# Second layer of two experts with 288 tokens: weights stationary, tokens moving, outputs transposed back on TensorE

## The chip, the cores and the metric

The kernel runs on 1 core of a Trainium2 chip. The metric is device time in microseconds (us) of one execution. Three runs of the kernel before took 524.7, 527.82 and 528.58 us; the median, 527.82, is its time.

## The reference, cut to what matters

Causal attention with 4 sink positions and a window of 128 over 4 batches, 8 heads, 768 positions and head size 64 gives x, 3072 tokens of 512 features. Then comes a mixture of experts: each token goes to one of 4 groups and in it to one of 4 experts, by the largest logit, so to one of 16.

```python
for g in range(G):            # 4 groups
    ...
    for e in range(Eg):       # 4 experts in each
        h = np.maximum(xg[mask_e] @ w1[g, e], 0.0)   # 512 -> 1024
        ye = h @ w2[g, e]                            # 1024 -> 512
        combined = g_w[mask_g][mask_e] * e_w[mask_e]
        out[tok_idx] = combined[:, None] * ye
```

Inputs and outputs are float32.

## The kernel before, in words

The first part of the span is attention and routing. From some 170 us on the experts are computed, in an order that depends on their load: an expert has a rank r by its number of tokens, and the rank has a fixed capacity, `CAPT[r]` (L44): 384, 256, 480, 288, 288, 224, ... tokens. Ranks 3 and 4 have 288. `GROUPS` (L49) pairs each with a small rank, its mate in this text: [3, 14] with 288 and 64 tokens, [4, 15] with 288 and 32. The group after each of them is one rank with 160 tokens (8 and 9). `PARTS` (L66) adds to each the offset `o`, the number of 128-token blocks `nt` (3 for 288), and `s`, the size of a rest of at most 64 tokens (32 for 288).

Every float32 product is made from three: each operand is split in a rounded part (hi) and a residual (lo), and hi x hi, hi x lo and lo x hi are added up. Weights arrive by DMA in chunks of 512 KB into `rw` (5 buffers); `wjob` (L668) casts one to `whi` on ScalarE and makes `wlo` on VectorE. There are 12 pairs of `whi` and `wlo`; a pair can be used again once its chunk has been counted in `state["freed"]`.

Layer 1 of a wide rank (`layer1_wide`, L921) has the weights stationary and the tokens moving: 8 steps of 128 hidden features, into a bank `ph` of PSUM (4 buffers) each. Under 240 tokens hi and lo of the tokens move together, and ScalarE copies half of the bank to `hc` and VectorE adds the other half to it; from 240 on there are three matmuls. `split_h` (L904) applies ReLU and splits the result into `hx` (hi on ScalarE, residual on VectorE). The mate's layer 1 (`layer1_narrow`) has the tokens stationary; its hidden layer `hs` is transposed on TensorE (`hidden_t`) while layer 2 of the large rank runs.

Layer 2 (`layer2`, L1001) has the tokens stationary and the weights moving, 512 columns wide: for each block of 128 tokens 8 steps of three matmuls into a bank `po` (2 buffers); the rest of 32 tokens has hi and lo side by side as 64 stationary columns, and so two matmuls a step. ScalarE scales the result by the gate into `ot` (3 buffers; for the rest VectorE adds the second half), and GpSimd scatters the rows to `out` by an indirect DMA.

The order of all instructions on each engine is the program's. The generators yield an estimate of PE time at each step; `spend` (L880) adds it to a clock and to a credit, and issues a weight cast when the credit reaches 1.8, a free pair is there and the planned landing of the raw chunk has passed. `pop_todo` (L995) issues in layer 2, at planned steps, the transposes of the mate's hidden layer and of the next group's inputs (`xpose`, L890). `fetch` (L1041) issues the gathers of inputs two groups ahead, on GpSimd's queue.

Of the kernel before, what the change touches and what calls it, by code (L numbers as in the profile page):

```python
# [9 lines left out]
F32 = mybir.dt.float32  # L10
# [4 lines left out]
AF = mybir.ActivationFunctionType  # L15
# [6 lines left out]
P = 128  # L22
# [4 lines left out]
DM = H * D  # L27
HP = H // 2
NDC = DM // P
G, EG, F = 4, 4, 1024  # L30
NE = G * EG
NFC = F // P
# [40 lines left out]
for _g in PARTS:  # L73
    _o = 0
    for _q in _g:
        _rem = _q["T"] % P
        _q.update(o=_o, nt=(_q["T"] + P - 1) // P, s=_rem if _rem <= 64 else 0)
        _o += 2 * _q["T"]
MAXB = 6
MAXA = 7  # L80
# [49 lines left out]
def moe_attention(tc, kqT, vN, vS, nsw, wgx, w1, w2, out):  # L130
    nc = Pinned(tc)
    v = nc.vector
    with ExitStack() as top, ExitStack() as att:
# [9 lines left out]
        ps_t = None  # L143
# [5 lines left out]
        def const(shape, dt, name):  # L149
            return cp.tile(shape, dt, name=name)  # L150
# [12 lines left out]
        hx = un[:, NDC * W:(NDC + NFC) * W].rearrange("p (f w) -> p f w", w=W)  # L163
# [3 lines left out]
        def bank(pt):  # L167
            return pt.tile([P, 4, P], F32, name="tp")
# [63 lines left out]
        ident = const([P, P], F32, "ident")  # L232
# [219 lines left out]
        start = const([P, NE], F32, "start")  # L452
# [173 lines left out]
        xg, cg, later = {}, {}, []  # L626
# [15 lines left out]
        state = dict(issued=0, done=0, freed=0, credit=0.0, route=0.0, clk=0.0, at=0.0, dma=0.0, gap=PELAG, dve=0.0)  # L642
# [25 lines left out]
        def wjob(force=False):  # L668
            if tail:
                prefetch(RAW)  # L670
            k = state["done"]
            if raws and not force and state["clk"] < raws[0][4]:
                return None
            if not raws or k >= state["freed"] + WBUF or (k % WBUF >= WA and len(wpool) < 2):
                return None
            l, r, c, rw, _ = raws.pop(0)
            wp = wpool[k % WBUF >= WA]
            hi = wp.tile([P, F], F32R, name="whi")
            lo = wp.tile([P, F], F32R, name="wlo")
            z = F if tail else F // 2  # L680
            nc.scalar.copy(hi[:, 0:z], rw[:, 0:z])

            def rest():
                v.tensor_tensor(lo, rw, hi.bitcast(F32), ALU.subtract)
                wt[l, r, c] = hi, lo
                if tail:
                    prefetch(RAW)
            dve(1.2)
            state["done"] += 1
            if tail:  # L690
                rest()
                return True

            def more():
                nc.scalar.copy(hi[:, z:], rw[:, z:])
                return rest

            half.append(more)
            return None
# [88 lines left out]
        po = ob[1].rearrange("p (c n) -> p c n", c=HP)  # L788
# [86 lines left out]
        def wait_for(key):  # L875
            while key not in ready:
                state["clk"] += 0.3
                routing(1)
# [36 lines left out]
        def weights(*k):  # L915
            while k not in wt:
                if not wjob(True):
                    raise RuntimeError("weights out of order")
            return wt[k]
# [75 lines left out]
        def pop_todo():  # L995
            plan["at"] += 1
            if plan["todo"] and plan["at"] >= plan["next"]:
                plan["next"] += plan["every"]
                plan["todo"].pop(0)()

        def layer2(q, j):  # L1001
            T, o, s, r = q["T"], q["o"], q["s"], q["r"]
            w = min(P, T - j * P)
            st = w if j * P + w > T - s else 0
            po = ps_o.tile([P, DM], F32, name="po")
            lastj = j == q["nt"] - 1
            for f in range(NFC):
                whi, wlo = (t[:, (f % 2) * DM:(f % 2 + 1) * DM] for t in weights(2, r, f // 2))
                hh = hx[:, f, o + j * P:o + j * P + w]
                a, z = f == 0, f == NFC - 1  # L1010
                if st:
                    hb = hx[:, f, o + j * P:o + j * P + 2 * w]
                    if z:
                        nc.tensor.matmul(po[0:w], hh, wlo, start=False, stop=False)
                    nc.tensor.matmul(po[0:2 * w], hb, whi, start=a, stop=z)
                    if not z:
                        nc.tensor.matmul(po[0:w], hh, wlo, start=False, stop=False)
                else:
                    hl = hx[:, f, o + T + s + j * P:o + T + s + j * P + w]
                    nc.tensor.matmul(po[0:w], hh, whi, start=a, stop=False)  # L1020
                    nc.tensor.matmul(po[0:w], hh, wlo, start=False, stop=False)
                    nc.tensor.matmul(po[0:w], hl, whi, start=False, stop=z)
                pop_todo()
                state["freed"] += 1 if q["last"] and lastj and f % 2 else 0
                yield 0.467 if st else 0.7
            jj = q["j0"] + j
            ot = yp.tile([P, DM], F32, name="ot", bufs=3)
            c = cg[r, jj]
            if q is PARTS[-1][-1] and j == 0:
                nc.scalar.activation(ot[:, 0:DM // 2], po[:, 0:DM // 2], AF.Copy, scale=c)  # L1030
                v.tensor_scalar(ot[:, DM // 2:], po[:, DM // 2:], c, None, ALU.mult)
            else:
                nc.scalar.activation(ot[0:w], po[st:st + w], AF.Copy, scale=c[0:w])
            if st:
                v.scalar_tensor_tensor(ot[0:w], po[0:w], c[0:w], ot[0:w], ALU.mult, ALU.add)
            cc = BASE[r] + jj
            nc.gpsimd.indirect_dma_start(
                out=out, out_offset=bass.IndirectOffsetOnAxis(ap=sidx[0:w, cc:cc + 1], axis=0),
                in_=ot[0:w], in_offset=None, bounds_check=N - 1, oob_is_err=False)

        def fetch(nxt):  # L1041
            for q in nxt:
                wait_for(f"x{q['r']}")
                for j in range(q["nt"]):
                    gather(q["r"], q["j0"] + j)

        def finish(g):
            for us in g:
                spend(us)
# [14 lines left out]
        for i in range(NI + 2):  # L1064
            live = i < NI
            a, b = i - 1, i - 2
            mid, old = 0 <= a < NI, 0 <= b < NI
            state["clk"] += 3.0
            if i == NI:
# [5 lines left out]
                ps_h = fl.enter_context(tc.tile_pool(name="ps_h", bufs=4, space=PSUM, side="right", reuse_waits="tile"))  # L1075
# [70 lines left out]
        ps_t = fl.enter_context(tc.tile_pool(name="ps_t", bufs=2, space=PSUM, side="left", reuse_waits="tile"))  # L1146
        ps_o = fl.enter_context(tc.tile_pool(name="ps_o", bufs=2, space=PSUM, side="left", reuse_waits="tile"))

        wpool.append(fl.enter_context(tc.tile_pool(name="wpb", bufs=WB, side="left", reuse_waits="tile")))
        yp = fl.enter_context(tc.tile_pool(name="yp", bufs=2, side="right", reuse_waits="tile"))  # L1150

        for i, g in enumerate(PARTS):
            nxt = PARTS[i + 1] if i + 1 < len(PARTS) else []
            if i == 1:
                fetch(nxt)
            todo = []
            for k, q in enumerate(g):
                plan.update(todo=todo, at=0, next=2, every=2)
                if i == 0 and k == 0:
                    finish(ew)  # L1160
                elif q["T"] > P:
                    finish(layer1_wide(q))
                else:
                    finish(layer1_narrow(q))
                    todo = todo + [lambda q=q, u=u: hidden_t(q, u) for u in range(2)]
            for f in todo if g[0]["T"] <= P else []:
                f()
                todo = []
            tot = NFC * sum(q["nt"] for q in g)
            if i == 0:  # L1170
                todo += [lambda: wait_for("x1"), lambda: None]
            todo += [lambda q=q, j=j: xpose(q, j) for q in nxt for j in range(q["nt"])]
            todo = [lambda fs=todo[k:k + 2]: [f() for f in fs] for k in range(0, len(todo), 2)]
            if i >= 1 and i + 2 < len(PARTS):
                fetch(PARTS[i + 2])
            first = 8 if len(g) > 1 else 2
            plan.update(todo=todo, at=0, next=first, every=(tot - first - 3) / max(1, len(todo)))
            if i == 0:
                plan.update(todo=todo[:1], next=2)
            for q in g:  # L1180
                for j in range(q["nt"])[::1 if i + 1 < len(PARTS) else -1]:
                    finish(layer2(q, j))
                if i == 0 and q["r"] == 0 and not q["last"]:
                    plan.update(todo=todo[1:], next=tot - 8, every=1.5)
            for f in plan["todo"]:
                f()
# [238 lines left out]
```

## Time and profile before

| | |
|---|---|
| median of three runs | 527.82 us |
| profiled execution | 523.2 us, span 521.5 us |
| PE (matmul) busy | 496.1 us, 95% |
| DVE (VectorE) busy | 384.5 us, 74% |
| ACT (ScalarE) busy | 346.9 us, 67% |
| POOL (GpSimd) busy | 157.0 us, 30% |

PE is the row of matmuls, PEld that of weight loads. Matmuls overlap in a pipeline, so a matmul's price is the distance between starts, not the length of its record. In a row "out<-in" the stationary operand of a matmul is shown with its partitions and columns ("128*64"), the moving one with its shape ("128x512"). The releaser of a wait is inferred.

### The profile page before, as it was taken

Reading aid. Unit: us, or ns where it says so; the run is one execution under the profiler, and the core shown is the slowest. Engines: PE = TensorE matmul, PEld = TensorE weight load, DVE = VectorE, ACT = ScalarE, POOL = GpSimd, SP = SyncE. Lnnn points to the kernel's source line nnn. Section 1 sums busy time; section 2 is a strip of 40 time slices with the busy share of each in tenths; the row PEclk is TensorE's granted clock in tenths of the full one; section 3 lists DMA queues with packets and bytes.
Section 4 is the critical chain, followed back from the end, with each engine's and each line's share of the span. In section 5 each row is a group of like instructions: output and inputs, shape, how many; then the busy total and the mean of one; then the engine's idle time right before and its main releaser. Section 6 shows DMA issues by size and latency. Waiting matters only on the chain.

```text
span 521.5 us, 14745 instructions
## 1 busy us (share of the span) xinstructions
PE 496.1 (95%) x5400; PEld 418.8 (80%) x5400; DVE 384.5 (74%) x1184; ACT 346.9 (67%) x900; POOL 157.0 (30%) x272
## 2 busy tenths in 40 slices
PE   8999899899898999999999999999999999999992
PEld 6778778788677988989889869787879797979781
DVE  7466896898987789984175769856988888788640
ACT  4889788798785445772374777755787777687530
POOL 3453453463465011413203021220352031203010
PEclk9999999999999999999999999999999999999996
DMA  7676768688885635895238488858877987598100
GB/s 229 208 209 226 216 195 234 206 277 228 240 265 162 192 121 194 303 318 225 67 105 302 134 263 299 304 165 301 293 253 272 323 288 251 202 314 302 53 5 27
DMA packets 50001, 114.34 MB, mean 219 GB/s; under 512 B 9486, under 2 KB 9486, under 8 KB 49920
## 3 DMA queue, kind: packets, MB, share of 16 engines
q1 hardware_dynamic: 45568, 100.25, 59.9%
q0 software_dynamic: 4352, 13.06, 6.9%
q8 instruction: 45, 0.74, 0.6%
q14 instruction: 36, 0.29, 0.2%
HBM read 100.69 MB, written 13.05 MB: 218 GB/s over the span
## 4 chain that ended last, share of the span: by engine, by line
PE 65%; DVE 1%; ACT 0%; issue 0%; POOL 0%; POOLq 0%; ACTq 0%
PE po L100 33%; PE ph L100 29%; PE tp L100 3%; DVE un L100 0%; DVE wlo L100 0%; ACT whi L100 0%; DVE lt L100 0%; POOL out L100 0%; DVE xt L100 0%; PE lg L100 0%; DVE req L100 0%; ACT xT L100 0%; DVE rm L100 0%; POOLq L1189 0%; DVE ot L100 0%
## 5 line engine op out<-in xcount | busy, mean ns | idle before, releaser
L100 DVE TENSOR_TENSOR wlo<-rw,whi 128x1024 fp32r<-128x1024 f32 x128 | 153.4, 1219 | 35.9 <-ACT whi L100 35.3
L100 PE MATMUL po<-whi,un 128*128 128x512 f32 (+2 forms) x448 | 151.8, 398 | 0.0
L100 ACT CAST whi<-rw 128x1024 fp32r<-128x1024 f32 (+1 forms) x132 | 131.7, 1023 | 18.7 <-DMA rw<-in_w 13.9
L100 PE MATMUL ph<-un,whi 128*128 128x256 f32 (+4 forms) x576 | 131.8, 316 | 0.6 <-DVE un L100 0.5
L100 POOL DMA_INDIRECT out<-ot,sidx x33 | 41.9, 1268 | 241.1 <-ACT ot L100 143.7
L100 PE MATMUL po<-wlo,un 128*128 128x512 f32 (+3 forms) x264 | 103.0, 395 | 0.0
L100 PE MATMUL ph<-un,wlo 128*128 128x160 f32 (+4 forms) x416 | 100.6, 267 | 0.0
L100 PEld LDWEIGHTS po<-whi,un 128*128 128x128 f32 (+2 forms) x448 | 80.3, 179 | 25.1
L100 PEld LDWEIGHTS ph<-un,whi 128*128 128x128 f32 x576 | 94.4, 189 | 2.9 <-DVE un L100 0.7
L100 ACT ACTIVATE pt<-sm,st 128x136 f32<-128x136 f32 x192 | 75.7, 400 | 16.1 <-DVE st L100 16.1
L100 PEld LDWEIGHTS ph<-un,wlo 128*128 128x128 f32 x416 | 77.1, 189 | 0.8
L100 PEld LDWEIGHTS po<-wlo,un 128*128 128x128 f32 (+3 forms) x264 | 43.4, 164 | 14.0
L100 DVE CUSTOM_DVE_ANT_0 sm<-ps,msk 128x136 f32<-128x136 f32 x192 | 45.7, 295 | 5.8 <-PE ps L100 1.8
L100 ACT ACTIVATE ot<-po,cg 128x512 f32<-128x512 f32 (+4 forms) x33 | 22.4, 679 | 34.2 <-PE po L100 25.6
L100 POOL DMA_INDIRECT xg<-xd,gidx x33 | 34.6, 1049 | 32.4 <-DVE key L100 20.8
L100 PE MATMUL ps<-kb,qb 64*64 64x216 f32 (+1 forms) x768 | 38.9, 339 | 1.1 <-DVE st L100 0.9
L100 DVE TENSOR_TENSOR hc<-ph,hc 128x160 f32<-128x160 f32 (+2 forms) x64 | 22.1, 346 | 24.2 <-ACT hc L100 23.9
L100 ACT ACTIVATE un<-ph 128x256 fp32r<-128x256 f32 (+1 forms) x40 | 15.7, 395 | 32.7 <-PE ph L100 32.2
L100 ACT ACTIVATION_READ_ACCUMULATOR pt<-sm,st 128x1 f32 x192 | 36.9, 192 | 0.0
L100 PE MATMUL po<-pa,vv 128*64 128x64 f32 x768 | 31.3, 223 | 3.9 <-issue 3.3
L100 ACT COPY hc<-ph 128x160 f32<-128x160 f32 (+2 forms) x64 | 19.9, 311 | 19.7 <-PE ph L100 12.4
L100 PEld LDWEIGHTS ps<-kb,qb 64*64 64x64 f32 x768 | 26.5, 132 | 7.4 <-DVE st L100 1.4
(190 smaller groups left out, 723.2 us busy)
## 6 DMA issues: line engine op xcount, KB each, us to landing
rw<-in_w SPq DMA_DIRECT2D x128, 512.0 KB, 5.2
vv<-in_vN SPq DMA_DIRECT2D x24, 512.0 KB, 5.8
kb<-in_kqT SPq DMA_DIRECT2D x24, 288.0 KB, 4.5
qb<-in_kqT SPq DMA_DIRECT2D x24, 256.0 KB, 4.0
xd<-xt SPq DMA_DIRECT2D x24, 256.0 KB, 3.6
svr<-in_vS SPq DMA_DIRECT2D x4, 192.0 KB, 4.6
xg<-xd,gidx POOLq DMA_INDIRECT x33, 4.7
out<-ot,sidx POOLq DMA_INDIRECT x33, 5.3
```

Of the source, the lines that this page charges most:

```text
L100: r = f(*a, **k)
```

## The change

Ranks that have between 240 and 384 tokens and a rest over a multiple of 128 get the mark `tr`; only ranks 3 and 4 do. For them `s` is 0, so residuals lie in one stretch, and a new generator, `layer2_cols`, takes the place of `layer2`. It makes the output with features on partitions: 4 passes c over 128 output features, each with 8 steps f of three matmuls with 128 weight columns stationary and 288 tokens moving, into a `ph` bank. ScalarE copies each pass to SBUF; three of these strips lie in an `hs` tile, the fourth in an `ot` tile. Then TensorE transposes 128x128 blocks back, four for each block of tokens (nine of the first three strips, and then three of the fourth), into the two `po` banks and one bank `tp`; ScalarE scales each into `ot`, and GpSimd scatters it. The mate's layer 2 follows in the old form.

```diff
-        _q.update(o=_o, nt=(_q["T"] + P - 1) // P, s=_rem if _rem <= 64 else 0)
+        _q["tr"] = 240 < _q["T"] < 384 and _rem > 0
+        _q.update(o=_o, nt=(_q["T"] + P - 1) // P, s=_rem if _rem <= 64 and not _q["tr"] else 0)
...
+        def layer2_cols(q):
+            T, o, r = q["T"], q["o"], q["r"]
+            yw = yp.tile([P, F], F32, name="hs", bufs=2)
+            yl = yp.tile([P, DM], F32, name="ot", bufs=3)
+            y = [yw[:, c * T:(c + 1) * T] for c in range(NDC - 1)] + [yl[:, 0:T]]
+            for c in range(NDC):
+                ph = ps_h.tile([P, 512], F32, name="ph")
+                for f in range(NFC):
+                    cs = slice(f % 2 * DM + c * P, f % 2 * DM + (c + 1) * P)
+                    whi, wlo = (t[:, cs] for t in weights(2, r, f // 2))
+                    hh, hl = hx[:, f, o:o + T], hx[:, f, o + T:o + 2 * T]
+                    a, z = f == 0, f == NFC - 1
+                    nc.tensor.matmul(ph[:, 0:T], whi, hh, start=a, stop=False)
+                    nc.tensor.matmul(ph[:, 0:T], whi, hl, start=False, stop=False)
+                    nc.tensor.matmul(ph[:, 0:T], wlo, hh, start=False, stop=z)
+                    if (c * NFC + f) % 4 < q["nt"]:
+                        pop_todo()
+                    state["freed"] += 1 if c == NDC - 1 and f % 2 else 0
+                    yield 0.4
+                nc.scalar.copy(y[c], ph[:, 0:T])
+            tx = [ps_o.tile([P, DM], F32, name="po").rearrange("p (a b) -> p a b", a=NDC) for _ in range(2)]
+            tx.append(bank(ps_t))
+            ws = [min(P, T - j * P) for j in range(q["nt"])]
+            for cs in (range(NDC - 1), range(NDC - 1, NDC)):
+                for j, w in enumerate(ws):
+                    for c in cs:
+                        nc.tensor.transpose(tx[j][0:w, c], y[c][:, j * P:j * P + w], ident)
+            for j, w in enumerate(ws):
+                ot = yp.tile([P, DM], F32, name="ot", bufs=3)
+                c = cg[r, q["j0"] + j]
+                nc.scalar.activation(ot[0:w], tx[j][0:w].rearrange("p a b -> p (a b)"), AF.Copy, scale=c[0:w])
+                scatter(r, q["j0"] + j, w, ot)
+            yield 1.2
...
             for q in g:
+                if q["tr"]:
+                    finish(layer2_cols(q))
+                    continue
                 for j in range(q["nt"])[::1 if i + 1 < len(PARTS) else -1]:
                     finish(layer2(q, j))
```

`scatter` is the indirect DMA that stood at the end of `layer2`, made a function.

## Rows read from the trace of the kernel before

**Rows 1.** The page, parts 1 and 2: busy time; granted clock in 40 slices

```profile
PE 496.1 (95%) x5400; PEld 418.8 (80%) x5400; DVE 384.5 (74%) x1184; ACT 346.9 (67%) x900; POOL 157.0 (30%) x272
...
PEclk9999999999999999999999999999999999999996
```

**Rows 2.** The chain of waits from 235 us on: shares by line

```profile
by line: PE po L100 48.8%; PE ph L100 43.2%; PE tp L100 4.7%; POOL out L100 0.3%; POOLq L1189 0.2%; DVE ot L100 0.2%; ACT ot L100 0.2%; issue 0.0%
```

**Rows 3.** Windows: length, busy time (count) of PE, PEld, DVE, ACT, POOL; clock, DMA

```profile
293.41:310.07 16.66, 16.66 (x81) 12.18 (x80) 12.13 (x17) 11.40 (x16) 1.29 (x1) 1.00 0.82 272
310.07:313.81 3.74, 3.74 (x18) 2.58 (x17) 3.74 (x5) 3.61 (x5) 1.72 (x1) 1.00 0.85 226
313.81:322.36 8.55, 8.55 (x66) 8.33 (x64) 7.92 (x21) 5.67 (x17) 0.89 (x1) 1.00 0.97 359
349.82:366.50 16.68, 16.68 (x82) 12.14 (x81) 11.88 (x17) 11.27 (x16) 1.68 (x2) 1.00 0.84 272
```

**Rows 4.** Timeline of PE (start, length): layer 1 of rank 4, first, next layer's first

```profile
333.30 0.43 PE L100 MATMUL ph<-un,whi 128*128 128x288 f32 x2
...
346.10 0.40 PE L100 MATMUL ph<-whi,un 128*64 128x512 f32 x1
```

**Rows 5.** Transposes: mean length of a record by form; eight together in PE's timeline

```profile
L100 PE MATMUL tp<-ident,xg 128*128 128x128 f32 x72 | 10.1, 272 | 0.0
...
306.83 0.95 PE L100 MATMUL tp<-ident,xg 128*128 128x128 f32 x8
307.72 0.44 PE L100 MATMUL po<-whi,un 128*64 128x512 f32 x1
```

**Rows 6.** Timeline of ACT, both groups (in brackets: idle before, and releaser)

```profile
285.07 0.41 ACT L100 ACTIVATE un<-ph 128x288 fp32r<-128x288 f32 x1 [1.19 <-PE ph L100]
...
305.69 0.69 ACT L100 ACTIVATE ot<-po,cg 128x512 f32<-128x512 f32 x1 [2.92 <-issue]
...
310.91 2.93 ACT L100 CAST whi<-rw 128x1024 fp32r<-128x1024 f32 x3
314.05 0.69 ACT L100 ACTIVATE ot<-po,cg 64x512 f32<-64x512 f32 x1 [0.22 <-ACT whi L100]
...
355.99 1.05 ACT L100 CAST whi<-rw 128x1024 fp32r<-128x1024 f32 x1 [2.20 <-DMA rw<-in_w]
```

**Rows 7.** The tile ot: landing of its scatters; POOL's timeline, both groups

```profile
DMA to landing us min/median/max: 2.2/5.3/7.7
...
303.04 1.29 POOL L100 DMA_INDIRECT out<-ot,sidx  x1 [17.88 <-ACT ot L100]
310.98 1.72 POOL L100 DMA_INDIRECT out<-ot,sidx  x1 [6.64 <-ACT whi L100]
318.68 0.89 POOL L100 DMA_INDIRECT out<-ot,sidx  x1 [5.98 <-DVE un L100]
324.19 0.92 POOL L100 DMA_INDIRECT out<-ot,sidx  x1 [4.62 <-DVE un L100]
...
359.43 1.30 POOL L100 DMA_INDIRECT out<-ot,sidx  x1 [16.95 <-ACT ot L100]
366.12 2.96 POOL L100 DMA_INDIRECT out<-ot,sidx  x1 [5.39 <-ACT whi L100]
```

**Rows 8.** Timeline of DVE: layer 1 of rank 8 and what is before it

```profile
315.81 0.73 DVE L100 SCALAR_TENSOR_TENSOR ot<-po,cg,ot 64x512 f32<-64x512 f32 x1
316.47 0.30 DVE L100 TENSOR_TENSOR hc<-ph,hc 128x160 f32<-128x160 f32 x1
...
318.05 0.32 DVE L100 TENSOR_TENSOR hc<-ph,hc 128x160 f32<-128x160 f32 x1
...
320.85 0.32 DVE L100 TENSOR_TENSOR hc<-ph,hc 128x160 f32<-128x160 f32 x1
```

**Rows 9.** Timeline of PE: the same layer 1, a usual pair and the last step

```profile
318.80 0.49 PE L100 MATMUL ph<-un,whi 128*128 128x320 f32 x2
...
320.88 0.75 PE L100 MATMUL ph<-un,whi 128*128 128x320 f32 x2
```

More of the change, by code (lines that the diff above doesn't have):

```diff
@@ L1035, in layer2, with scatter @@
                 v.scalar_tensor_tensor(ot[0:w], po[0:w], c[0:w], ot[0:w], ALU.mult, ALU.add)
+            scatter(r, jj, w, ot)
+        def layer2_cols(q):
[31 more added lines that the diff above has]
+            yield 1.2
+        def scatter(r, jj, w, ot):
             cc = BASE[r] + jj
```

## The prediction

> **The bound.** Read the page's busy shares first: TensorE (PE) is busy 95% of the 521.5 us, at the upper clock level (2.4 GHz; nines in the clock strip) in all slices but the last [rows 1]. A busy share does not show that an engine sets the end, so the chain of waits comes next. From 235 us on its pieces are matmuls and transposes, 48.8 + 43.2 + 4.7 = 96.7% by line, with no other engine above 0.3% [rows 2]. So in this half a microsecond saved on PE is worth one, and a wait put in front of PE costs one. Then look at the stretches that the change touches: with windows from the first matmul of the 288-token second layer to the first of its group mate's, PE is busy for all of 16.66 us in the first group (experts of ranks 3 and 14) and 16.68 us in the second (4 and 15) [rows 3]. The profiled execution took 523.2 us, 4.6 below the 527.82 of the median; I work with differences and add them to the median.
>
> **PE's work.** Before, layer 2 of 288 tokens is 24 + 24 + 16 = 64 matmuls with 512 columns. The mate's sixteen of the same width take 3.74 us, 0.234 each [rows 3]; 64 make 14.96 us. The other 1.70 us of the window are 16 transposes that were there before and stay (hidden layer of the mate, inputs of the next group).
> After, it is 4 x 8 x 3 = 96 matmuls with 288 columns. Layer 1 of the rank-4 expert is just that, the same order of weights (hi, hi, lo) included: from 333.30 to 346.10, 12.80 us for 96, 0.133 each [rows 4]. Added are 12 transposes; the eight that stand together take 307.72 - 306.83 = 0.89 us, 0.111 each [rows 5], so 1.33. By work alone a window becomes 12.80 + 1.70 + 1.33 = 15.83, a gain of 0.83 us.
> That transpose price needs a caution. Each record lasts 0.27 us [rows 5]; the eight are cheap because records overlap. The Trainium skill, page "TensorE: Matmul & The Clock Gate", Part 4: PE-mode transpose, puts a 128x128 transpose at about 275 ns in a kernel's context; twelve of those would cost 3.3 us and turn the gain to a loss of 1.1. Here the row decides, 0.111; a rival below takes the other price.
>
> **ScalarE's part.** Four copies of 128x288 from PSUM are added; the ReLU of that shape takes 0.41 [rows 6], so 1.6 us of ScalarE (ACT), and three of the copies lie under the 3.2 us of the next pass's matmuls. The fourth does not: PE needs it for the last three transposes, and ACT works in order. Which casts stand ahead of it follows from the planner. A cast needs a free weight pair; layer 2's pairs are given back only in the last of the four passes, at its 2nd, 4th, 6th and 8th step, while credit has piled up. So three casts are issued in that pass, ahead of the copy. Times from the first matmul: three passes 9.60, the mate's transposes 0.80, one step 0.40, the transposes of inputs 0.89, one step 0.40, makes 12.1; with the end of the pipelined matmul 12.25. Three casts back to back take 2.93 [rows 6]: 15.2. Copy 0.41: 15.6. Meanwhile PE ended its matmuls at 14.5 and nine transposes at 15.5, so it waits only about 0.1. The first of the last transposes ends 0.27 later, 15.87.
> Next wait: the mate's layer 2 wants a bank of `po`, and both banks hold the transposed output. The first is free after ACT's scaling, 0.69 [rows 6]: 16.56. So PE starts the mate at about 16.6 instead of 16.66. The gain of 0.83 is spent on two waits, net -0.05 per expert. Bounds: with no cast in the way the copy is ready before PE, and the mate starts at 16.4 (-0.25); if a cast there waits for its raw weights as one did for 2.20 us [rows 6], +2.1. I take -0.05, since the three casts before were not held so.
>
> **Output tiles.** Here is the cost that I expect. `ot` has three buffers. The new function takes one for its fourth strip and three for its results, so the mate's result is the fourth after the strip and gets the buffer of the first result, which must have been scattered. Before, it got the buffer of the first of three results, two blocks of matmuls older. How long does a scatter hold? Landing has a median of 5.3 and at most 7.7 us [rows 7]. Stronger are the starts on POOL: the second output of rank 3 was scaled by 306.38 [rows 6], yet its scatter starts at 310.98, and then 318.68 and 324.19: 7.94, 7.70 and 5.51 apart, with an unrelated releaser named; in the second group 359.43 to 366.12 is 6.69 [rows 7]. One scatter waits for the one before; so its hold, counted from its start, is 5.5 to 7.9. For a group's first scatter, which is the one in question, the rows give 7.94 and 6.69.
> First result ready 16.56, scatter starts 0.27 later, 16.84; buffer free at 23.5 to 24.8 (5.5: 22.3). The mate's layer 2 takes 3.74, so the next layer 1 (160 tokens) starts at about 20.34. ACT would scale the mate's output then, 0.24 after that start as before (314.05 against 313.81) [rows 3, 6]; now it stands at the head of its queue until 3.2 to 4.4 after it. Behind it are the copies `hc` that empty `ph`, and behind its own adding step on VectorE (DVE) the additions that free `ph`. There are four `ph` banks; one step of layer 1 lasts (8.55 - 0.27)/8 = 1.035, so step 5 wants bank 1 back at 4.14.
> Bank 1 comes free after scaling 0.69, adding step 0.66 and addition 0.30 [rows 6, 8]: 4.85 to 6.05, 0.7 to 1.9 late. Step 6 then waits too: a weight split sits between the first two additions, which start 1.58 apart [rows 8], 0.54 more than a step. The planner counts a window as 32 x 0.4 + 1.2 = 14.0 us instead of 16 x 0.7 + 8 x 0.467 = 14.9 and comes out of it with more credit; by its rules the second cast in that layer 1 moves one step earlier, so the third addition has one ahead of it too: another 0.54. The trace of before has a stall of this kind already, where PE's last step waits for the addition at 320.85 and a pair of matmuls lasts 0.75 instead of 0.49 us, some 0.27 lost [rows 8, 9]. Sum: 0.7 + 1.08 - 0.27 = 1.5 to 1.9 + 1.08 - 0.27 = 2.7 us per expert. With the short hold it is 0.4. I take 2.7 for the first group and 1.5 for the second, by each group's own row: 4.2 in all.
>
> **No cost.** One residual instruction per hidden chunk instead of two and the missing addition of the 32-token output free DVE, which isn't in the chain. All weights of layer 2 are wanted within the first pass, 3.2 us instead of 5.6; the planner has issued their casts before the mate's layer 1 ends, so if a cast were late PE would wait for it there. Three results at once make POOL's scatters queue, about 7 us later each, and the input gathers behind them too; those inputs are transposed in the layer 2 of a later group, and if that cover fails PE waits for them.
>
> **Sum.** 2 x (-0.05) + 4.2 = +4.1 us: 527.3 against the profiled 523.2, 531.9 against the median.
>
> **Rivals.** My forecast is slower, by 0.8%.
> *The ring is covered.* If a scatter holds its buffer under 5.5 us, or the four banks swallow the delay, stalls come to -0.27 to +0.4, and the windows to about the same: -0.6 to +0.8 in all, 527.2 to 528.6. For it: only two first scatters show the hold. Against it: the bank ring already stalls at 0.27.
> *Not slower: PE's work alone counts.* The copy is early, the eviction and the ring are hidden: 2 x -0.83 = -1.7, 526.1. This decides if ACT reaches the copy before PE's nine transposes end; against it, both `po` banks are taken and nothing of PE's stands between.
> *Slower by more than 1%: ACT's queue jams.* At the end of layer 2 a cast waits for raw weights (2.20 each time) and pushes copy, eviction, scatter and ring alike: 4.1 + 2 x 2.1 = +8.3, 536.1. It decides when a raw tile lands after 12 us of the window. For: that wait is in the trace; against: earlier in the window.
> *Transposes at their full records.* 12 x 0.27 - 1.33 = 1.9 more per expert if they don't overlap, +7.9, 535.8. The page named above speaks for it; its own sum without waits is in the sentence there. Against: rows 5.
>
> **Chances.** Forecast 0.50, covered ring 0.25, PE's work alone 0.08, jam 0.13, full records 0.04. About 1%, 5.3 us, is what a measurement here can tell from no change: above 533.1 or below 522.5. The forecast's own range is +1 to +6, 528.8 to 533.8, and a fifteenth of it passes the bound. So slower 0.13 + 0.04 + 0.03 = 0.20; faster 0.02, for two gains of 0.83 cannot reach 5.3 and only an unforeseen shift of the planner could; same 0.78. The range reaches from PE's work alone less a little spread of the runs (524.7 to 528.58) to the jam: 525.5 to 536.
>
> **What would show it.** In the new trace: 96 matmuls of 288 columns in `ph<-whi,un` order at 0.133; a PE gap of 0.7 to 0.9 before the mate's first matmul, released by ACT's scaling; the mate's scaling on ACT starting 3 to 4 us into the next layer 1; stalls of PE there at steps 5 to 7. If that scaling starts within 1 us, the ring step is wrong and the time stays; if the copy of the fourth strip follows matmuls by under 0.5 us, the order of casts is.

## Result, and the profile after

The changed kernel takes 532.06 us (median of 4 runs, 528.38 to 534.13) against 526.26 for the kernel before in all its runs of that set. The ratio is 1.0101, with a 95% interval of 1.0056 to 1.0147: slower by 1%. Timed again it was 1.0115 (1.0069 to 1.0162). Some executions of any of these kernels are slow, over 1.5% above its fastest; the ratios here leave them out, and the first profiles of the two controls at the end, which fell on such ones, are read only in windows where the granted clock is 1.00.

The profiled executions differ by 528.38 - 523.2 = 5.2 us. Where these lie is read from windows over a whole group, from the first matmul of the 288-token layer 1 to the first one after the next group's layer 1. Columns are those of [rows 3]: length, busy time of PE, PEld, DVE, ACT and POOL, clock, DMA. First the kernel before:

```profile
276.88:322.36 45.48, 45.48 (x274) 38.47 (x272) 31.86 (x60) 28.66 (x49) 8.86 (x8) 1.00 0.75 252
333.30:378.67 45.37, 45.36 (x273) 37.21 (x272) 32.77 (x62) 29.49 (x50) 9.04 (x7) 1.00 0.78 265
```

The same two windows of the kernel after:

```profile
277.60:325.19 47.59, 45.50 (x317) 41.70 (x316) 31.23 (x53) 30.13 (x53) 7.89 (x8) 1.00 0.73 242
336.14:383.84 47.70, 45.52 (x317) 40.49 (x316) 32.20 (x55) 30.03 (x54) 7.11 (x8) 1.00 0.76 257
```

They are 2.11 and 2.33 us longer, 4.44 together. The rest of the 5.2, 0.72, was there before the first of them begins (277.60 against 276.88), in a part of the program that the change doesn't touch; between 120 and 160 us the granted clock was 0.96 after and 1.00 before. PE, busy for the whole of both windows before, now stands idle for 47.59 - 45.50 = 2.09 and 2.18 us in them. The granted clock is 1.00 in all four, the 2.4 GHz level.

Cut further, into layer 2, the mate's layer 2, and the next layer 1 (first group, then second), after:

```profile
294.12:311.63 17.51, 16.24 (x126) 15.25 (x124) 13.60 (x18) 12.23 (x20) 0.00 (x0) 1.00 0.78 250
311.63:315.43 3.80, 3.80 (x16) 2.68 (x17) 1.93 (x3) 3.80 (x5) 1.02 (x1) 1.00 0.97 285
315.43:325.19 9.76, 8.95 (x65) 8.39 (x64) 8.08 (x23) 6.12 (x17) 1.89 (x2) 1.00 0.89 317
352.66:370.21 17.55, 16.20 (x125) 15.27 (x123) 13.42 (x18) 12.02 (x20) 0.00 (x0) 1.00 0.75 252
370.21:373.98 3.77, 3.77 (x17) 2.05 (x18) 1.91 (x3) 3.77 (x5) 1.03 (x1) 1.00 0.79 267
373.98:383.84 9.86, 9.03 (x65) 8.39 (x64) 8.12 (x23) 6.16 (x17) 1.90 (x2) 1.00 0.93 318
```

The new layer 2 isn't shorter but 0.85 and 0.90 us longer than the old one, which took 16.66 and 16.65 (the second window of it in [rows 3] ends 0.03 behind the mate's first matmul, at 366.47). The next layer 1 went from 8.55 [rows 3] to 9.76 and from 8.56 to 9.86. The mate's own layer 2 between them is only 0.06 and 0.13 longer. So there are two losses: one inside the new function, and one a whole layer behind it.

The timeline of PE after shows the first (start, length, instruction, in brackets idle time and releaser):

```profile
298.18 0.46 PE L101 MATMUL tp<-ident,hs 64*128 64x64 f32 x4
299.35 0.46 PE L101 MATMUL tp<-ident,hs 64*128 64x64 f32 x4 [0.71 <-DVE hs L101]
...
309.55 0.82 PE L101 MATMUL po<-ident,hs 128*128 128x128 f32 x6
310.21 0.49 PE L101 MATMUL tp<-ident,hs 128*32 128x128 f32 x3
310.53 0.42 PE L101 MATMUL po<-ident,ot 128*128 128x128 f32 x2
310.80 0.27 PE L101 MATMUL tp<-ident,ot 128*32 128x128 f32 x1
311.63 0.49 PE L101 MATMUL po<-whi,un 128*128 128x512 f32 x1 [0.56 <-ACT ot L101]
```

The mate's hidden layer is transposed at the 8th planned step. That used to be 5.69 us into layer 2 (299.10); now it is 4.06. DVE's last sum into `hs`, which these transposes read, ends where it did, 5.23 us into layer 2 before and 5.17 after (first row before, second after):

```profile
297.96 0.68 DVE L100 TENSOR_TENSOR hs<-hs,ph 64x512 f32<-64x512 f32 x1
298.62 0.67 DVE L101 TENSOR_TENSOR hs<-hs,ph 64x512 f32<-64x512 f32 x1
```

So the second four of the eight transposes find it unfinished, and PE is idle for 0.71 us (0.79 in the second group). At the end the twelve transposes follow each other from 309.55 on, and then PE is idle for 0.56 us, waiting for ACT to empty the bank that the mate needs.

ACT and POOL after, at the same place:

```profile
307.23 2.95 ACT L101 CAST whi<-rw 128x1024 fp32r<-128x1024 f32 x3
310.08 0.39 ACT L101 COPY ot<-ph 128x288 f32<-128x288 f32 x1
310.89 1.27 ACT L101 ACTIVATE ot<-po,cg 128x512 f32<-128x512 f32 x2 [0.42 <-PE po L101]
312.04 0.66 ACT L101 ACTIVATE ot<-tp,cg 32x512 f32<-32x512 f32 x1
312.61 2.92 ACT L101 CAST whi<-rw 128x1024 fp32r<-128x1024 f32 x3
317.85 0.69 ACT L101 ACTIVATE ot<-po,cg 64x512 f32<-64x512 f32 x1 [2.31 <-DMA out<-ot,sidx]
```

```profile
311.85 1.02 POOL L101 DMA_INDIRECT out<-ot,sidx  x1 [25.95 <-ACT ot L101]
318.55 1.00 POOL L101 DMA_INDIRECT out<-ot,sidx  x1 [5.67 <-ACT ot L101]
323.69 0.89 POOL L101 DMA_INDIRECT out<-ot,sidx  x1 [4.13 <-ACT hc L101]
328.93 1.48 POOL L101 DMA_INDIRECT out<-ot,sidx  x1 [4.35 <-DVE un L101]
```

The last row of ACT is the second loss. Before, the mate's scaling started 0.24 us after the next layer 1 ([rows 6], 314.05); now it starts 317.85 - 315.43 = 2.42 after it, released by the scatter of the first result, which began at 311.85. All three results were ready by 312.70 and the mate's by 319.31, and still the scatters start 6.70, 5.14 and 5.24 apart: one at a time.

In the chain of waits after, that scatter has become a link; for its 5.89 us, and until PE's seventh step, PE isn't in the chain:

```profile
311.85 5.89 DMA out<-ot,sidx
...
317.85 0.07 ACT ot L101
...
318.56 0.29 ACT hc L101
318.85 0.96 ACT whi L101
...
320.98 0.32 DVE hc L101
...
321.59 1.14 DVE wlo L101
322.73 0.25 DVE hc L101
...
323.02 2.34 PE ph L101 x16
```

DMA, scaling, copy `hc`, a cast, its split, an addition, a second split, an addition, and then PE's seventh step. PE's own rows say the same:

```profile
320.55 0.35 PE L101 MATMUL ph<-un,whi 128*128 128x320 f32 x1
321.35 0.42 PE L101 MATMUL ph<-un,whi 128*128 128x320 f32 x1 [0.45 <-DVE hc L101]
321.61 0.24 PE L101 MATMUL ph<-un,wlo 128*128 128x160 f32 x1
```

From the last matmul of a step to the second of the next is 0.33 us where nothing waits (step 4, 318.36 to 318.69). In front of steps 5, 6 (the rows above) and 7 it is 0.46, 1.06 and 0.96, so these come 0.13, 0.73 and 0.63 late; of the last two PE is idle for 0.45 and 0.36, released by DVE `hc`. Together that is 1.49; less the 0.27 that was lost there before [rows 8, 9], it is 1.22, and this layer 1 grew by 1.21.

### The profile page after: what moved, and what is told of

Same layout as the page of the kernel before. It is cut to its first block, busy times and chain, and to the rows that moved or that the text cites. A ratio compares the mean times of both kernels' runs of the same rounds, so it can differ in the third digit from the quotient of the medians.

```text
span 526.7 us, 14903 instructions
## 1 busy us (share of the span) xinstructions
PE 496.6 (94%) x5488; PEld 425.8 (81%) x5488; DVE 382.7 (73%) x1166; ACT 349.6 (66%) x908; POOL 156.8 (30%) x272
## 5 line engine op out<-in xcount | busy, mean ns | idle before, releaser
L101 PE MATMUL ph<-un,whi 128*128 128x288 f32 (+4 forms) x704 | 158.6, 313 | 2.4 <-DVE hc L101 1.6
L101 PE MATMUL po<-whi,un 128*128 128x512 f32 (+2 forms) x368 | 125.4, 399 | 1.1 <-ACT ot L101 1.1
L101 PEld LDWEIGHTS ph<-un,whi 128*128 128x128 f32 x704 | 115.3, 189 | 5.9 <-DVE hc L101 2.7
L101 PE MATMUL ph<-un,wlo 128*128 128x288 f32 (+4 forms) x480 | 119.4, 271 | 0.0
L101 POOL DMA_INDIRECT out<-ot,sidx x33 | 40.7, 1232 | 246.1 <-ACT ot L101 164.6
L101 PEld LDWEIGHTS ph<-un,wlo 128*128 128x128 f32 x480 | 89.1, 189 | 0.9
L101 PE MATMUL po<-wlo,un 128*128 128x512 f32 (+3 forms) x216 | 84.3, 395 | 0.0
L101 PEld LDWEIGHTS po<-whi,un 128*128 128x128 f32 (+2 forms) x368 | 66.2, 180 | 21.9 <-ACT ot L101 1.7
L101 PEld LDWEIGHTS po<-wlo,un 128*128 128x128 f32 (+3 forms) x216 | 35.7, 165 | 11.1
L101 ACT ACTIVATE ot<-po,cg 128x512 f32<-128x512 f32 (+4 forms) x31 | 20.9, 680 | 33.3 <-PE po L101 26.5
```

Of the source, the lines that this page charges most:

```text
L101: r = f(*a, **k)
```

## The experiments

Group spans are the windows above: first group, second group, and their sum against 45.48 + 45.37 = 90.85 before. Each row is one profile.

| kernel | first | second | sum - before | timed ratio to before (95%) |
|---|---|---|---|---|
| changed | 47.59 | 47.70 | +4.44 | 1.0101 (1.0056 to 1.0147) |
| changed, again | 47.48 | 47.60 | +4.23 | 1.0115 (1.0069 to 1.0162) |
| four `ot` buffers | 46.15 | 46.13 | +1.43 | 1.0042 (1.0002 to 1.0082) |
| later transposes of the mate | 46.94 | 46.74 | +2.83 | 1.0017 (0.9977 to 1.0058) |
| a free bank for the mate | 47.80 | 47.73 | +4.68 | 1.0053 (1.0025 to 1.0082) |
| all three | 44.85 | 44.80 | -1.20 | 0.9978 (0.9934 to 1.0022) |
| all three, again | 44.84 | 44.80 | -1.21 | 1.0006 (0.9971 to 1.0041) |
| strip in its own tile | 47.68 | 47.63 | +4.46 | not timed |
| before, four `ot` buffers | 45.35 | 45.22 | -0.28 | 1.0050 (1.0007 to 1.0092) |
| before, two `ot` buffers | 48.20 | 48.20 | +5.55 | 1.0034 (0.9993 to 1.0076) |

Where a kernel was profiled twice, the spans of the table repeat to 0.1 or so (two `ot` buffers excepted, see below); the total doesn't. In these profiles the first group begins anywhere between 276.7 and 286.9 us, after a first part that is the same code in all. The control with four buffers shows what that does: its groups are as before, and its ratio is 1.005. So mechanisms are read from the spans here, and of the ratios only those of the changed kernel and of all three edits together are used, each measured twice.

**Four buffers.**

```diff
-            yl = yp.tile([P, DM], F32, name="ot", bufs=3)
+            yl = yp.tile([P, DM], F32, name="ot", bufs=4)
```
(and so at the other two places of `ot`)

> The changed kernel with four ot buffers instead of three. Ring theory: the mate's scaling on ACT starts within 0.5 us of the next layer 1's first matmul instead of 2.4 after it, both layer 1 of 160 tokens fall from 9.76 and 9.86 us to 8.5 to 8.7, and the time falls by about 2.4 us (0.45%). Rival, casts and splits alone fill ACT and DVE there, the ring only hides behind them: both layer 1 stay above 9.3 and the time changes by less than 0.8 us.

The mate's scaling starts at 314.86, 0.26 us after the next layer 1 begins (314.60), and waits only for PE. Both layer 1:

```profile
314.60:322.89 8.29, 8.29 (x65) 8.29 (x64) 8.03 (x24) 6.13 (x17) 1.41 (x1) 1.00 0.99 352
371.65:379.94 8.29, 8.29 (x66) 8.29 (x64) 8.08 (x24) 6.20 (x17) 1.31 (x1) 1.00 0.91 346
```

PE is busy without a gap, and both are below even the 8.55 of before. The spans fall by 3.01 us, 0.6 more than expected. The ring theory holds; the same casts and splits are still there.

**Later transposes of the mate.**

```diff
+            if g[0]["tr"]:
+                plan.update(next=12, every=6.5)
```

With `next` at 12, `every=6.5` leaves the transposes of the inputs at the planned step where they were.

> The changed kernel with the transposes of the mate's hidden layer issued at the 12th planned step of layer 2 instead of the 8th, all else as it is. Theory: they come 2 us too early in the shorter layer 2 and wait for DVE's sum hs (0.71 and 0.79 us idle); moved, the gap is gone, layer 2 of 288 tokens to the mate's first matmul falls from 17.42 and 17.48 us to 16.6 to 16.8, and the time falls by 1.5 us, as scatter and ring move with it. Rival, the wait turns up at the copy of the fourth strip or in the mate's split: less than 0.5 us.

Layer 2, first and second group, and the next layer 1 of the first:

```profile
299.14:315.75 16.61, 16.05 (x125) 15.20 (x124) 13.74 (x18) 12.23 (x20) 0.00 (x0) 1.00 0.79 265
357.02:373.60 16.58, 16.02 (x125) 15.19 (x123) 13.43 (x18) 12.07 (x20) 0.00 (x0) 1.00 0.80 266
319.59:329.56 9.97, 9.08 (x66) 8.39 (x64) 8.04 (x23) 6.08 (x17) 1.92 (x2) 1.00 0.92 319
```

Layer 2 falls by 0.90 and 0.97 from its 17.51 and 17.55 (the 17.42 and 17.48 of the expectation end 0.09 and 0.07 before the mate's first matmul). The gap in front of the transposes is gone and the spans fall by 1.61 in all, as expected; the ring's loss stays.

**A free bank for the mate.**

```diff
-            tx = [ps_o.tile(...) ... for _ in range(2)]
-            tx.append(bank(ps_t))
+            tx = [ps_o.tile(...) ... for _ in range(1)]
+            tx += [bank(ps_t), bank(ps_t)]
```

> The changed kernel with the transposed outputs in one po bank and two tp banks, so that the mate finds a po bank free. Theory: the mate starts 0.7 us earlier, but the buffer of ot comes free at the same moment, so the next layer 1 grows by the same 0.6 to 0.7 us and the time stays within 0.4 us. Rival, the waits add up independently: 1.4 us less.

```profile
299.78:316.50 16.72, 16.00 (x126) 15.28 (x124) 12.85 (x18) 11.52 (x18) 0.00 (x0) 1.00 0.79 254
320.31:331.06 10.75, 9.09 (x66) 8.40 (x64) 8.88 (x24) 6.92 (x17) 1.90 (x2) 1.00 0.86 306
```

The mate starts 17.51 - 16.72 = 0.79 us earlier, and the next layer 1 is 10.75 - 9.76 = 0.99 longer: nothing gained, +0.24 over both groups. The scaling of the mate's result is released 23.93 us after layer 2 began, against 23.73 in the changed kernel. So the wait ended at nearly the same moment, and what PE saved ahead of it was given back there.

**All three.** The three edits together.

> Four ot buffers, transposes of the mate at the 12th step and two tp banks for the outputs, together. Theory: with the ring gone the free bank counts too; 2.4 + 1.5 + 1.4 = 5.3 us less than the changed kernel, 0.5 to 1.5 us below the kernel before; layer 2 to the mate's first matmul is 15.8 to 16.0 us. Rival, a next wait (copy of the fourth strip behind the casts) keeps 1 us or more per expert: not below the kernel before.

```profile
300.51:316.32 15.81, 15.81 (x126) 15.22 (x124) 12.76 (x18) 11.52 (x18) 0.00 (x0) 1.00 0.79 269
356.30:372.08 15.78, 15.78 (x125) 15.22 (x124) 12.63 (x18) 11.34 (x18) 0.00 (x0) 1.00 0.83 272
320.13:328.83 8.70, 8.56 (x66) 8.33 (x64) 8.70 (x24) 6.96 (x17) 1.17 (x1) 1.00 0.97 341
```

Layer 2 is 15.8 us with PE busy throughout. The spans fall by 5.64 against the changed kernel and end 1.20 below the kernel before. The first two edits alone gave -3.01 and -1.61, 4.62 together; the bank, which alone gave +0.24, brings the other 1.02, 0.5 per expert and not the 0.7 that was expected. In layer 2 it gives 0.80 (16.61 to 15.81), but layer 1 of the first group takes 8.70 instead of the 8.29 with four buffers alone: the mate's scaling now stands behind three casts on ACT until 321.07, 0.94 us into that layer. The timed ratio shows no gain over the kernel before, 0.9978 with an interval that holds 1.000. The same kernel once more:

> Four buffers, later transposes and the free bank, once more. Theory: group spans of 44.8 us, 0.2% under the kernel before and 1.0% under the changed one. Rival, the first part decides: no difference to the changed kernel beyond 0.4%.

The spans came out at 44.84 and 44.80; the ratio was 1.0006, not 0.998. The rival, no difference to the changed kernel beyond 0.4%, fell: that one ran on the same chip beside it and read 1.0115. The two ratios lie 1.1% apart, some 5.7 us, and the spans 4.23 + 1.21 = 5.44. So here the timed runs confirm the spans.

> The changed kernel itself, once more, beside the next run on the same chip. Theory: group spans of 47.6 and 47.7 us wherever the first part of the program ends, and 0.8% (4.4 us) over the kernel before. Rival, part of the 1% lies in the first part of the program: group spans as said, but a ratio under 1.004.

Spans 47.48 and 47.60 and a ratio above 1.004: the 1% is real, and 4.2 to 4.4 us of it lie in the two groups. Where the rest lies in the timed runs isn't shown.

**The strip apart.**

```diff
-            yl = yp.tile([P, DM], F32, name="ot", bufs=3)
+            yl = yp.tile([P, DM], F32, name="yl", bufs=1)
```

> The changed kernel with the fourth strip in a tile of its own, three ot buffers. Theory: the mate's result is still the third after the first result and gets its buffer, so ACT waits 2.3 us for the DMA as before and both groups take 47.6 to 47.8 us. Rival, it is the strip's buffer that is missing: the wait goes and each group falls by 1.4 us, as with four buffers.

```profile
322.55 0.69 ACT L101 ACTIVATE ot<-po,cg 64x512 f32<-64x512 f32 x1 [2.38 <-DMA out<-ot,sidx]
```

The wait is 2.38 us (2.31 with the strip in the ring), and the spans are the same. It isn't the strip that uses up the ring; three results at one moment do.

**The wait without the new function.** The kernel before with two `ot` buffers, and with four as a control; each got a second profile.

> The kernel before with two ot buffers instead of three: the wait alone, without the new layer 2. The mate's result now gets the buffer of the second result, whose scatter starts 3 us before it is wanted. Ring theory: ACT waits about 4 us there for the DMA, the next layer 1 of 160 tokens grows from 8.55 to between 10.2 and 11.5 us in both groups, and the time grows by 4 to 6 us (0.8 to 1.1%). Rival, the wait is swallowed by the four ph banks: both layer 1 stay under 9 and the time within 1 us.

```profile
323.38 0.69 ACT L100 ACTIVATE ot<-po,cg 64x512 f32<-64x512 f32 x1 [3.80 <-DMA out<-ot,sidx]
```

Both layer 1:

```profile
319.55:330.82 11.27, 9.07 (x66) 8.39 (x64) 8.00 (x21) 5.57 (x17) 3.05 (x3) 1.00 0.82 277
378.57:389.96 11.39, 9.07 (x65) 8.39 (x64) 8.11 (x21) 5.66 (x17) 1.77 (x2) 1.00 0.74 272
```

ACT waits 3.80 us for the scatter, and layer 1 grows by 2.7 and 2.8, with layer 2 untouched. So in this execution the ring alone does it, without the new function. The expected 4 to 6 us of time did not show: the ratio is 1.0034, and the upper end of its interval, 1.0076, is 4.0 us, less than the 5.55 of the spans (1.1%). The spread of the first part may hide some of it, but not all of it is there in every run: the fastest one took 525.64, only 3.17 above the fastest of the kernel before beside it, 522.47. The two profiled executions took 534.49 and 533.0 us; how long the wait is in the others isn't known.

> The kernel before with four ot buffers: a control. Ring theory: nothing waits there for a buffer of ot, so both groups take 45.4 us as they are, within 0.2. Rival, any fourth buffer speeds the kernel up, for another reason: 1 us less in each group, as the fourth buffer gave the changed kernel.

> The kernel before with four ot buffers, one more profile: group spans of 45.2 to 45.5 us by the ring theory; 44.4 if any fourth buffer helped.

45.35 and 45.22, again 45.36 and 45.21: the kernel before has no wait to lose there.

> The kernel before with two ot buffers, one more profile: group spans of 48.0 to 48.4 us and an ACT wait for the DMA of about 4 us by the ring theory; 45.4 if the banks swallow it.

The wait was 4.08 us and the spans 49.32 and 48.53. The first of them has a granted clock of 0.97 in the window and isn't used; the second is 0.1 over what was expected and 0.33 over the first profile.

## Why the prediction was right

The time was forecast at 531.9 and measured at 532.06. That they are so near is luck, in two ways. The forecast started from 527.82, the median of three runs of the kernel before, which is 526.26 with a fourth; the change itself was forecast at +4.1 and measured at +5.8 by the medians, +5.2 between the profiles and +4.44 in the two groups. And of that sum two terms were off, by about the same amount and to opposite sides: layer 2 by about +1.8 us and the ring by -1.7. The mechanism that the forecast put first, the ring, is still the larger of the two losses.

- **PE's work** was right. 96 matmuls and 28 transposes were to take 15.83 us; with the waits taken away they take 15.81 and 15.78. The twelve new transposes stand between 309.55 and about 310.9, 0.11 each. The rival that took the full records is out. The Trainium skill ("TensorE: Matmul & The Clock Gate", Part 4: PE-mode transpose) has about 275 ns for one (of bf16; here they are float32): that agrees with the length of a record here (272 ns), not with the price in a row of them.
- **The fourth strip's copy** came as forecast behind three casts (2.95 us, forecast 2.93), and ended at 310.47, just before PE wanted it at 310.53: no wait, where 0.1 was forecast. The forecast's sign for a wrong order of casts, a copy under 0.5 us behind the matmuls, would have misled: the copy starts 0.37 behind them (309.71), with the three casts in front of it all the same. The jam by raw weights didn't come.
- **The bank of `po`**: a gap of 0.7 to 0.9 was forecast in front of the mate; PE is idle for 0.56 there, and a free bank starts the mate 0.79 earlier.
- **Layer 2's net** failed: -0.05 per expert forecast, +0.85 and +0.90 measured. The step that failed is the one that counted the mate's transposes as work that stays and asked nothing about when they come. They are planned by counting steps; with shorter steps they come 1.6 us earlier, and the sum `hs` on DVE, which moved by less than 0.1, was late by then. Moving them brought layer 2 to 16.61 and 16.58, which is the forecast's 16.6.
- **The ring** was right in kind, in place and in what releases what, and mis-sized: 4.2 us forecast, 1.21 + 1.30 = 2.51 in the two layer 1. Two steps of its sum were wrong. The forecast took the distance between starts on POOL as the time that a scatter holds its buffer, 7.94 and 6.69 us; the hold was 5.89 and 5.95, while the starts are 6.70 and 6.80 apart in the new trace. The starts say when the next scatter could go, and that may have waited for more than the first. Of the rows at hand 5.5 was nearest; the forecast's own sum with it comes to 0.3 per expert, not the 0.4 that it names. With the measured start of the mate's scaling, 2.42 after layer 1's first matmul, the forecast's own formula gives a bank free at 2.42 + 1.65 = 4.07 against the 4.14 wanted; step 5 was late by 0.13, where 0.7 to 1.9 was forecast. The other wrong size goes the other way: steps 6 and 7 were to be 0.54 late each and were 0.73 and 0.63. They are two, so the second cast that moves one step earlier was right. Removing the ring gave more than these 2.51, 3.01, since the old stall of 0.27 in each group [rows 8, 9] went as well.
- **The rivals**: the covered ring would have left layer 1 at 8.55 or so, and it took 9.76 and 9.86; PE's work alone shows only with three further edits.

What was not settled: why one scatter waits for the one before it. That ready tiles wait is in the trace after, with 5.1 to 6.7 us between starts; that it is the scatter before which they wait for is read from this and not tested, for no experiment here changed it.

## What to carry to other kernels

A rewrite that makes a stage's own work shorter also moves its results in time: three outputs that used to be spread over a stage now come at once, and a ring of buffers that nothing waited for becomes the longest wait. Before such a change, write down for each buffer ring who gets which buffer and how long its last reader holds it, and for each piece of work that is planned by counting steps, when those steps now come. And a saving ahead of a wait that ends at a fixed time is worth nothing until the wait is gone: the free bank gave +0.24 us alone, and -1.02 with the other two.

## What the runs showed of the hardware that was not expected

A control whose two groups took the same time as before (90.57 against 90.85 us) was timed at 1.005 with an interval that leaves out 1.000, and a kernel with 5.55 us more in its groups at 1.0034. The start of the first group, after code that is the same in all of these kernels, lay between 276.7 and 286.9 us. Part of that may be TensorE's granted clock: between 40 and 80 us it was 1.00 in the kernel before, at the 2.4 GHz level, and 0.87, a mean of both levels, in the first profile of all three edits, whose first group starts at 283.98. It can't be the whole: the second profile of that kernel has 1.00 up to its first group and still starts it at 280.01. What else moves it is open.

What follows the two groups, 142.8 us long before, took 143.3 and 143.4 in the two profiles of the first control, so about 0.5 us of its 0.5% (2.6 us) can be the edit's. For the rest, an interval of half a percent says how well the ratio repeats for that program, not that the edit caused it; for that, the windows around the edit are the better measure, as long as they repeat in a second profile and the timed runs don't contradict them.
